# Attention in units of two batches by 64 tokens: one score tile, one value tile, two TensorE tasks per unit

## The chip, the cores and the metric

The kernel runs on one core of one Trainium2 chip. The metric is the time of one execution on the device in microseconds. Everything is float32 on the outside; the big matrix products are split into a high and a low part and run as three products each.

## The reference

The program is a linear-attention layer followed by a two-layer network. The attention keeps a state of 48 by 48 for each batch and head and walks over 768 tokens:

```
for t in range(S):                                  # B, H, S, D = 4, 8, 768, 48
    cur = einsum('bhd,bhe->bhde', u * kt, vt)
    y[:, :, t] = einsum('bhd,bhde->bhe', rt, state + cur)
    state = wt[..., None] * state + einsum('bhd,bhe->bhde', kt, vt)
x = y.transpose(0, 2, 1, 3).reshape(B * S, H * D)   # 3072 x 384
h = x @ w_in                                        # 384 x 2048
g = where(h > 0, h, exp(min(h, 0)) - 1)
out = g @ w_out                                     # 2048 x 384
```

## The kernel before, in words

The tokens are cut into six chunks of 128 (`NC = 6`). A unit is one chunk of one batch, so there are 24 units, four to a chunk. The network (called MLP below) runs once per chunk, over the 512 columns that the four units make, in 16 steps `f` of 128 hidden rows. A step is a block `g1` (9 matmuls of 128x512 into the tile `ph`, L238), two ScalarE passes and a VectorE pass for the nonlinearity (`r1`, `r2` L243 and L246, `stt` L249), the split into high and low (`gh` L253, `gl` L257), and a block `g2` (9 matmuls into three accumulators `acc`, L268). In the chunks 0 and 1 the first six steps run in two halves of 256 columns (`FH`), so that the network can begin when two units are done.

A unit of attention has these steps. VectorE makes the products of the decays from both ends of the segment by two scans (`e_scan` L377, `g_scan` L387) and multiplies them into r and k (`r_hat` L392, `k_hat` L396). The diagonal term u·r·k comes from TensorE in the units 0 to 7 (`diag_pe` L421) and from GpSimd in the others (L404, L407, then `diag` L411); it is spread to a diagonal matrix `am`, by eight ScalarE instructions in the units 0 to 7 (`spread_act` L432) and by GpSimd afterwards (`spread` L442). TensorE makes the scores (`score` L456, tile `pa_s`), VectorE copies the part above the diagonal into `am` (`mask` L460). TensorE transposes k (`trans` L465), ScalarE copies that out (L469). The values (`value`, L493 to L506) are the sum of the old state times r (`state_part`) and of v times `am`; ScalarE and VectorE take them out as the high and low part of x (`x_high` L513, `x_low` L519). The new state is k times v (`outer` L532), added to the decayed state (`scale_state` L472, `update` L540, for chunk 0 a copy, L542).

A unit comes in two forms. In the chunks 0, 1 and 5 the segment is 128 tokens long: scores of 128x128, the state part with contraction over 112 rows, then the product of k and v. In the chunks 2, 3 and 4 (`HALVES`) the unit is done in two segments of 64 tokens, one after the other: the scores are 64x64 in four corners of the array, and the state is updated twice, so that the order is `trans` and `score`, then `outer` and the state part of the first segment, then (after `update` and `scale_state`) the state part of the second segment and the masked values of both. In PSUM three banks (`SLOTS["pa"] = 3`) serve all of this: scores take two, a transpose one, values one or two. The state is stored as 96 columns per pair of heads (`st`, L326), of which each half of the rows uses 48 and the others stay zero, so that both heads of a pair are contracted at once over 112 rows.

The order of the work is written by a planner in the kernel (`Plan.order`, L94). It knows each task's engine, an estimated duration (`COST`), what it waits for, the buffers it takes, and due times derived from `BEGINS` (the start of each chunk's network). It simulates the engines, and the order it finds is issued as it stands: every engine then works its list in that order, and an instruction whose input is late holds up everything behind it on the same engine. Loads and stores stand in one list on SP. A guard (`guard` L579: a small matmul, two VectorE instructions) checks that the scans kept in range; a slow path behind a branch (`general`) runs if not.

The weights are converted at the start: 16 steps, each with one VectorE pass `conv_and` L563, two shifts L567 and L571, the low part L577, and two ScalarE passes L559 and L574.

Of the kernel before, what the change touches and what calls it, by code (L numbers as in the profile page):

```python
# [19 lines left out]
P = 128  # L20
C = 128
# [7 lines left out]
HC = C // 2  # L29
CWS = 2 * NP * (HC + 1)  # L30
W1, K1, R1 = CWS + 1, NP * C, NP * C
WKR = dict(w=(0, W1), k=(W1, W1 + K1), r=(W1 + K1, W1 + K1 + R1))
NU = NC * B
FH = (6, 6)
# [19 lines left out]
COST = dict(es=1.5, gs=1.4, pc=0.2, pd=0.6, md=0.22, spa=2.4, rh=0.62, kh=0.62, rk=0.48, rku=0.48, prk=1.1, prku=1.1, dg=0.5, mk=0.7, up=0.7, sc=0.5, xl=0.48,  # L54
            cand=0.5, cv=0.9, wl=0.9, stt=0.6, gl=0.64, fl=1.4, kt=0.5, xh=0.46, a=0.87, wh=0.8, r1=0.58, r2=0.6, gh=0.6,
            sp=1.7, s=1.15, t=0.5, v=1.75, v0=1.1, u=0.5, g=2.06, out=0.6, sh=0.6, ya=0.4, vh=1.0)
LAT = 0.06
DMA_FIRST, DMA_ISSUE, DMA_LAT, DMA_RATE = 1.0, 0.45, 1.9, 215.0
BEGINS = (20.9, 120.4, 207.5, 284.8, 361.5, 453.5, 461.1)
SOON = 0.0  # L60
HALF = 0.0
STAY = 0.0
SWITCH = 0.0
MODES = dict(s=1, v=2, u=3, pd=4)
STAG = 10.9
STAG_C = 0.0
HALVES = (2, 3, 4)
FIRST = "DVE"
FILL = {}
COLS = 128  # L70
PAD = 96
# [3 lines left out]
SLOTS = dict(w=2, k=3, r=3, rk=2, v=4, eg=2, md=2, am=2, kt=1, pa=3, wg=2, ph=2, m=2, gh=2, gl=2, x=2, acc=1, raw0=1, x0=1, x1=1, x1a=1, x1b=1)  # L75


class Plan:
# [15 lines left out]
    def order(self):  # L94
# [29 lines left out]
        server, mode = DMA_FIRST, None  # L124
# [5 lines left out]
        while len(order) < len(ts):  # L130
            moved = False
            for e in ready:
# [3 lines left out]
                for k in ready[e]:  # L136
# [6 lines left out]
                    u = (t["late"] + (STAY if e == "PE" and (k[0] in MODES) != (mode in MODES) else 0.0), rank[k])  # L143
# [22 lines left out]
                end = now + t["dur"] * (2.0 if e == "PE" and now < HALF else 1.0)  # L166
                if e == "PE":
                    end += SWITCH * (MODES.get(mode, 0) != MODES.get(k[0], 0))
                    mode = k[0]
# [46 lines left out]
ROUNDS = value_rounds()  # L216


def mlp(nc, w_h, w_l, ps_acc, ps_h, ml, gp, po, dst, last=False):
# [9 lines left out]
    def g1(s, x, fill=()):  # L229
# [3 lines left out]
        for m in fill:  # L233
            nc.tensor.matmul(ph[:, 0:P], m, m, start=True, stop=True)
# [57 lines left out]
def rwkv_elu_kernel(ctx, tc, wkr, rk, vp, u, uz, gkrw, gv, gu, w_in, w_out, out):  # L292
# [16 lines left out]
    ps_a = pool("ps_a", 3, space=PS)  # L309
# [10 lines left out]
    upper = kp.tile([P, C], F32, name="upper")  # L320
    upper_h = kp.tile([P, HC], F32, name="upper_h")
    upper_h4 = upper_h.bitcast(U32).unsqueeze(1).broadcast_to([P, 4, HC])
    upper4 = upper.bitcast(U32).unsqueeze(1).broadcast_to([P, 4, C])
# [4 lines left out]
    for u_ in units:  # L328
        u_["L"] = HC if u_["half"] else C
        u_["S"] = NP * C // u_["L"]  # L330
    spans = lambda x, u_: x.rearrange("d (s t) -> d s t", s=u_["S"])
    scan = lambda x, u_, z: spans(x[:, z, 0:u_["S"] * (u_["L"] + 1)], u_)
    raws, xts = {}, {}

    def set_reset(eng, u_):
        eng.memset(reset, 2.0 ** -62)
        eng.memset(scan(reset, u_, 0)[:, :, u_["L"]:u_["L"] + 1], 1.0)

    def constants():
        nc.scalar.preload_act_table_set("natural_log_exp_and_others")  # L340
        set_reset(nc.vector, units[0])
        nc.vector.memset(lim, -(2.0 ** 60))
        make_identity(nc, ident)
        nc.vector.memset(upper, 1.0)
        nc.gpsimd.affine_select(out=upper, in_=upper, pattern=[[1, C]], compare_op=ALU.is_gt,
                                fill=0.0, base=0, channel_multiplier=-1)
        nc.vector.memset(upper_h, 1.0)
        for z in range(2):
            nc.gpsimd.affine_select(out=upper_h[HC * z:HC * z + HC], in_=upper_h[HC * z:HC * z + HC], pattern=[[1, HC]], compare_op=ALU.is_gt,
                                    fill=0.0, base=0, channel_multiplier=-1)  # L350
        nc.gpsimd.memset(st, 0.0)
        nc.vector.memset(ones_c, 1.0)

    def warm():
        pw = ps_a.tile([P, P], F32, tag="pa", name="pw")
        for _ in range(WARM):
            nc.tensor.matmul(pw, ident, ident, start=True, stop=True)
# [4 lines left out]
    def load(u_, n):  # L362
        c, b = u_["c"], u_["b"]
        if n in WKR:
            lo, hi = WKR[n]
            t, src = ld.tile([R2, hi - lo], F32, tag=n, name=n, bufs=SLOTS[n]), wkr[c, b, :, lo:hi]
        elif n == "rk":
            t, src = ld.tile([P, 2, DM], F32, tag=n, name=n, bufs=SLOTS[n]), rk[c, b]
        else:
            t, src = ld.tile([P, 4 * P], F32, tag=n, name=n, bufs=SLOTS[n]), vp[c, b]  # L370
# [3 lines left out]
    def e_scan(u_):  # L374
        u_["eg"] = eg = at.tile([R2, 2, CWS], F32, tag="eg", name="eg", bufs=SLOTS["eg"])
        n = u_["S"] * (u_["L"] + 1)
        nc.vector.tensor_tensor_scan(out=eg[:, 0, 0:n][:, ::-1], data0=u_["w"][:, 1:n + 1][:, ::-1], data1=reset[:, 0, 0:n][:, ::-1],  # L377
                                     initial=0.0, op0=ALU.mult, op1=ALU.max)

    def decay(u_):  # L380
        u_["pc"] = at.tile([R2, 2 * NP, 1], F32, tag="pc", name="pc", bufs=6)[:, 0:u_["S"]]
        nc.scalar.copy(u_["pc"], scan(u_["eg"], u_, 0)[:, :, 0:1])

    def g_scan(u_):
        n = u_["S"] * (u_["L"] + 1)
        nc.vector.reciprocal(scan(reset, u_, 1)[:, :, 0:1], scan(u_["eg"], u_, 0)[:, :, 0:1])
        nc.vector.tensor_tensor_scan(out=u_["eg"][:, 1, 0:n], data0=u_["w"][:, 0:n], data1=reset[:, 1, 0:n],  # L387
                                     initial=0.0, op0=ALU.mult, op1=ALU.max)

    def r_hat(u_):  # L390
        r = spans(u_["r"].rearrange("d p t -> d (p t)"), u_)
# [464 lines left out]
```

## Time and profile before

| what | value |
|---|---|
| median of three runs | 541.48 us (539.18 to 541.5) |
| span of the profiled execution | 540.9 us |
| TensorE matmul busy | 515.5 us (95%) |
| VectorE busy | 371.1 us (69%) |
| ScalarE busy | 285.8 us (53%) |
| GpSimd busy | 74.7 us (14%) |
| matmuls of the network, L238 and L268, of the chain that ended last | 34% and 33% |

The page of the profile cuts the span in 40 slices and gives each engine's busy share in tenths. A timeline row gives start, duration, engine, line, operation and shape (contraction rows times output rows, then operand), and how many instructions of one kind it joins. A matmul's duration in a row includes the way through the array, so consecutive rows overlap; what an instruction occupies is the distance from its start to the start of the next row. A float32 matmul shows as two records, a transpose and the network's matmuls as one. The chain of waits follows the work that ended last back in time.

### The profile page before, as it was taken

How to read it: one execution, taken by the hardware profiler on the slowest of the kernel's cores; microseconds unless marked ns; L12 is line 12 of the kernel's file. 1: busy time of each engine (PE TensorE's matmuls, PEld its weight loads, DVE VectorE, ACT ScalarE, POOL GpSimd, SP SyncE). 2: the span in 40 equal slices, each digit the busy share in tenths (PEclk: the TensorE clock that was granted, in tenths of full speed). 3: DMA queues.
4: the chain of work that ended last, by engine and by line, in shares of the span. 5: the costliest groups of instructions: out<-in, count | busy, mean ns of one | idle time of the engine just before them, and what ended most of it. 6: DMA issues, size and time to landing. Idle time of an engine off the chain costs nothing.

```text
span 540.9 us, 12202 instructions
## 1 busy us (share of the span) xinstructions
PE 515.5 (95%) x5121; PEld 427.7 (79%) x5121; DVE 371.1 (69%) x614; ACT 285.8 (53%) x570; POOL 74.7 (14%) x102
## 2 busy tenths in 40 slices
PE   6876999989999999999999999999999999999994
PEld 5666998878999777787777788777788887888883
DVE  5899899988778875469964478964436995333331
ACT  3768588675855453455453365543355543454441
POOL 2000000000243120028120035120031400000000
PEclk9977899979999999999999999999999999999998
DMA  8954754021562200094310083100084110010001
GB/s 243 287 176 141 226 175 164 19 56 35 175 178 76 65 2 2 2 263 133 85 33 2 3 241 103 35 2 3 1 254 124 48 35 2 0 60 0 1 0 63
DMA packets 26749, 47.54 MB, mean 88 GB/s; under 512 B 2753, under 2 KB 9281, under 8 KB 26689
## 3 DMA queue, kind: packets, MB, share of 16 engines
q1 hardware_dynamic: 26544, 46.58, 28.7%
q8 instruction: 42, 0.69, 0.5%
q14 instruction: 19, 0.15, 0.1%
q10 hardware_dynamic: 144, 0.13, 0.1%
HBM read 41.98 MB, written 4.72 MB: 86 GB/s over the span
## 4 chain that ended last, share of the span: by engine, by line
PE 80%; DVE 9%; DMA 6%; ACT 2%; issue 1%; SPq 0%; DVEq 0%; ACTq 0%
PE ph L238 34%; PE acc L268 33%; PE pa_s L456 3%; PE pa_y L501 3%; DMA v<-in_vp_dram 3%; PE pa_u L506 2%; PE pa_u L493 2%; PE pa_u L532 1%; DMA wrawx<-in_w_out_dram 1%; DMA rk<-in_rk_dram 1%; PE pa_t L465 1%; DVE eg L387 1%; DVE gl L257 1%; DMA k<-in_wkr_dram 1%; DVE r L392 1%
## 5 line engine op out<-in xcount | busy, mean ns | idle before, releaser
L243 ACT ACTIVATE m<-ph 128x512 f32<-128x512 f32 (+1 forms) x108 | 59.2, 549 | 132.8 <-PE ph L238 131.5
L249 DVE SCALAR_TENSOR_TENSOR m<-m,ph 128x512 f32<-128x512 f32 (+1 forms) x108 | 67.4, 624 | 84.7 <-ACT m L246 84.2
L238 PE MATMUL ph<-xh,w_h 128*128 128x512 f32 (+1 forms) x324 | 123.2, 380 | 2.0 <-ACT w_h L574 1.6
L238 PE MATMUL ph<-xh,w_l 128*128 128x512 f32 (+1 forms) x324 | 120.7, 372 | 3.7 <-DVE w_l L577 3.7
L268 PE MATMUL acc<-gh,w_h 128*128 128x512 f32 (+1 forms) x325 | 123.6, 380 | 0.0
L268 PE MATMUL acc<-gl,w_h 128*128 128x512 f32 (+1 forms) x325 | 120.2, 370 | 0.1
L238 PE MATMUL ph<-xl,w_h 128*128 128x512 f32 (+1 forms) x324 | 120.1, 371 | 0.0
L268 PE MATMUL acc<-gh,w_l 128*128 128x512 f32 (+1 forms) x325 | 119.9, 369 | 0.0
L257 DVE TENSOR_TENSOR gl<-m,gh 128x512 fp32r<-128x512 f32 (+1 forms) x108 | 73.2, 681 | 36.4 <-ACT gh L253 35.9
L253 ACT CAST gh<-m 128x512 fp32r<-128x512 f32 (+1 forms) x108 | 61.5, 571 | 55.9 <-DVE m L249 33.2
L238 PEld LDWEIGHTS ph<-xh,w_l 128*128 128x128 f32 x324 | 62.3, 192 | 15.0 <-DVE w_l L577 4.6
L238 PEld LDWEIGHTS ph<-xh,w_h 128*128 128x128 f32 x324 | 62.2, 192 | 14.3 <-ACT w_h L574 2.4
L268 PEld LDWEIGHTS acc<-gh,w_h 128*128 128x128 f32 x325 | 62.4, 192 | 12.8 <-issue 1.0
L268 PEld LDWEIGHTS acc<-gh,w_l 128*128 128x128 f32 x325 | 62.4, 192 | 10.2
L268 PEld LDWEIGHTS acc<-gl,w_h 128*128 128x128 f32 x325 | 62.5, 192 | 9.7 <-DVE gl L257 0.5
L238 PEld LDWEIGHTS ph<-xl,w_h 128*128 128x128 f32 x324 | 62.5, 193 | 9.4
L246 ACT ACTIVATE m<-m 128x512 f32<-128x512 f32 (+1 forms) x108 | 63.3, 586 | 2.9
L442 POOL TENSOR_SCALAR_AFFINE_SELECT am<-md 64x256 f32<-64x256 f32 (+1 forms) x56 | 30.5, 548 | 96.9 <-PE pa_u L493 61.9
L404 POOL TENSOR_TENSOR rk<-rk 128x384 f32<-128x384 f32 x16 | 19.1, 1192 | 134.1 <-DMA rk<-in_rk_dram 132.2
L377 DVE TENSOR_TENSOR_SCAN eg<-w,reset 112x516 f32<-112x516 f32 (+1 forms) x24 | 31.0, 1292 | 2.6 <-DMA w<-in_wkr_dram 2.6
L456 PE MATMUL pa_s<-r,k 48*64 48x64 f32 (+1 forms) x576 | 27.3, 262 | 5.5 <-ACT md L425 2.2
L401 ACT ACTIVATE junk<-eg,lim 112x1032 bf16<-112x1032 f32 (+1 forms) x24 | 27.7, 1153 | 8.2 <-DVE eg L387 8.2
(72 smaller groups left out, 513.4 us busy)
## 6 DMA issues: line engine op xcount, KB each, us to landing
v<-in_vp_dram SPq DMA_DIRECT2D x24, 256.0 KB, 6.5
rk<-in_rk_dram SPq DMA_DIRECT2D x16, 384.0 KB, 4.1
w<-in_wkr_dram SPq DMA_DIRECT2D x24, 227.9 KB, 3.9
k<-in_wkr_dram SPq DMA_DIRECT2D x24, 224.0 KB, 4.9
r<-in_wkr_dram SPq DMA_DIRECT2D x24, 224.0 KB, 5.3
out_dram<-o SPq DMA_DIRECT2D x17, 256.0 KB, 2.5
wrawx<-in_w_in_dram SPq DMA_DIRECT2D x10, 384.0 KB, 3.5
wrawx<-in_w_out_dram SPq DMA_DIRECT2D x10, 384.0 KB, 4.1
```

The lines of the kernel that those rows point to most:

```text
L238: nc.tensor.matmul(ph[z:z + COLS], w[:, f, 0, k, z:z + COLS], x_[:, k, :], start=(k == n == 0), stop=(k == NK - 1 and n == 2))
L243: act(s["m"], s["ph"], AF.Relu, scale=-1.0)
L246: act(s["m"], s["m"], AF.Exp, scale=-1.0)
L249: stt_(s["m"], s["m"], -1.0, s["ph"], ALU.add, ALU.max)
L253: nc.scalar.copy(s["gh"], s["m"])
L257: nc.vector.tensor_tensor(s["gl"], s["m"], s["gh"].bitcast(F32), ALU.subtract)
L268: nc.tensor.matmul(a_[z:z + COLS], w[:, f, 1, m, z:z + COLS], g[:, s_], start=(f == n == 0 and lo == 0), stop=(f == NF - 1 and q == parts ...
L377: nc.vector.tensor_tensor_scan(out=eg[:, 0, 0:n][:, ::-1], data0=u_["w"][:, 1:n + 1][:, ::-1], data1=reset[:, 0, 0:n][:, ::-1], initial=0. ...
L401: act(junk[:, :, 0:n], u_["eg"][:, :, 0:n], AF.Relu, bias=lim, accum_out=flags[:, u_["i"]:u_["i"] + 1])
L404: eng.tensor_tensor(u_["rk"][:, 0], u_["rk"][:, 0], u_["rk"][:, 1], ALU.mult)
L442: nc.gpsimd.affine_select(out=am[rs, :, 0:L], in_=u_["md"][rs, q::2].unsqueeze(2).broadcast_to([L, NP, L]), pattern=[[0, NP], [1, L]], com ...
L456: nc.tensor.matmul(pa[q][ts, p, 0:L], u_["k"][rs, p, ts], u_["r"][rs, p, ts], start=True, stop=True)
```

## The change

Every unit is now a pair of batches times 64 tokens. There are 12 steps in time of two units each, still 24 units, and four units still make one chunk of 512 columns. The two segments of a unit belong to two batches, so they do not depend on each other; the dependence runs from unit i to unit i+2, also within a chunk. The units 0 and 1 have no old state (`first`), the units 22 and 23 make no new one (`last`).

- One TensorE task `s` makes the transposes of k and the scores; one task `v` makes the state part, the masked values and the product of k and v. Before there were three or four tasks: `t`, `s`, `v`, `u`, and `ya` in the halved form.
- PSUM: a tile of two banks, one buffer (`pair`, tag `pa`), holds the scores, and then the values and the state product together; another tile of one bank, one buffer (`single`, tag `pb`), holds the transposes, the diagonal term, and the guard's sum. The task `s` takes both, `v` takes `pa` again after the mask, and holds it until `x_high`, `x_low` and `update` are done.
- The state is 80 columns wide (`st`), with 48 in use at the same place for both heads of a pair. The state part is contracted over the 48 rows of one head, 32 output rows at a time: 32 matmuls in place of 24, in two passes with a TensorE `drain` between them, since the second pass adds to the same PSUM places from the other half of the array's rows.
- One `mask`, one `x_high`, one `x_low`, one `scale_state` and one `update` instruction per unit, each over both segments. `update` of the units 0 and 1 is a copy on ScalarE. The spread on ScalarE writes 64 columns instead of 128 per instruction; GpSimd spreads with two instructions instead of four.
- The constants for both segment lengths, and the reset of them by GpSimd when the length changes, are gone. Costs, due times (`BEGINS`, a spacing `STAG` of 17 instead of 10.9) and the guard's due time are new; the guard's old due time lay behind those of the whole last chunk.
- The host lays the inputs out per unit; sizes of loads are the same.

```diff
-    st = cst.tile([R2, B, NP, 2 * D], F32, name="st")
-    units = [dict(c=i // B, b=i % B, i=i, half=i // B in HALVES) for i in range(NU)]
+    st = cst.tile([R2, B, NP, 80], F32, name="st")
+    sv = st[:, :, :, 16:16 + D]
+    units = [dict(c=i // B, b=(2 * (i % STEP), 2 * (i % STEP) + 1), i=i, first=i < STEP, last=i >= NU - STEP) for i in range(NU)]
...
+    def pair():
+        return ps_a.tile([P, 2, 512], F32, tag="pa", name="pa", bufs=1)
+
+    def single():
+        return ps_a.tile([P, 512], F32, tag="pb", name="pb", bufs=1)
...
     def score(u_):
-        u_["pa"] = pa = [ps_a.tile([P, NP, C], F32, tag="pa", name="pa_s") for q in range(2)]
...
+        if not u_["last"]:
+            u_["pt"] = pt = single()[:, 0:NP * R2].rearrange("t (p d) -> t p d", p=NP)
+            for p in range(NP):
+                nc.tensor.transpose(pt[:, p], u_["k"][:, p, :], ident[0:R2, 0:R2])
+        u_["pa"] = pa = pair()[:, :, 0:NP * L].rearrange("t q (p s) -> t q p s", p=NP)
...
+    def mask(u_):
+        nc.vector.copy_predicated(u_["am"], upper4, u_["pa"])
...
+    def scale_state(u_):
+        b = slice(u_["b"][0], u_["b"][0] + 2)
+        tt(sv[:, b], sv[:, b], u_["pc"].rearrange("d (p h) o -> d h p o", h=2).broadcast_to([R2, 2, NP, D]), ALU.mult)
+
+    def value(u_):
+        v, am, rp = u_["v"], u_["am"], u_["r"]
+        both = pair()
+        u_["pu"] = pu = both[0:R2, :, 0:NP * D].rearrange("d h (p e) -> d h p e", p=NP)
+        u_["py"] = py = both[:, :, NP * D:NP * D + NK * L].rearrange("d h (k t) -> d h k t", k=NK)
...
+        def state_part(swap):
+            for n in range(2 * NP):
+                for h in range(2):
+                    p, x = HEADS[h ^ swap][n]
+                    rs, e = slice(64 * (x // 2), 64 * (x // 2) + D), (16, 48, 0, 32)[x]
+                    mm(h, p, x, st[rs, u_["b"][h], p, e:e + 32], rp[rs, p, L * h:L * h + L])
+
+        if not u_["first"]:
+            state_part(1)
+            nc.tensor.drain()
+            state_part(0)
+        for p, x in ROUNDS:
+            for h in range(2):
+                rs = slice(L * h, L * h + L)
+                mm(h, p, x, v[rs, P * p + 32 * x:P * p + 32 * x + 32], am[rs, x // 2, p], stop=u_["last"] and (p, x) in ENDS)
+        if u_["last"]:
+            return
         for p in range(NP):
...
             for h in range(2):
+                rs = slice(L * h, L * h + L)
+                for z in range(2):
+                    m = 64 - 16 * z
+                    nc.tensor.matmul(pu[64 * z:64 * z + m, h, p], u_["kt"][rs, p, 64 * z:64 * z + m], v[rs, P * p + 80 * z:P * p + 80 * z + D],
+                                     start=False, stop=(p == NP - 1))
...
-        hold("pa", ("s", i), [("mk", i, 0), ("mk", i, 1)], 2, fifo=False)
...
+        hold("pa", ("s", i), [("mk", i)], fifo=False)
+        hold("pb", ("s", i), [("kt", i)], fifo=False)
+        hold("kt", ("s", i), [("v", i)])
+        hold("pa", ("v", i), [("xh", i), ("xl", i), ("up", i)], fifo=False)
...
-    add(("guard",), "PE", 0.3, guard, [("fl", i) for i in range(NU)], due=BEGINS[-2] + 15)
+    add(("guard",), "PE", 0.3, guard, [("fl", i) for i in range(NU)], due=BEGINS[-2] + 10.0)
```

More of the change, by code (lines that the diff above doesn't have):

```diff
@@ L33 @@
 NU = NC * B
+STEP = B // 2
 FH = (6, 6)
@@ L165, in order @@
                         users.setdefault(x, []).append(h)
[L166 to L169, printed above, removed]
+                end = now + t["dur"]
                 busy[e] = end
@@ L216 @@
 ROUNDS = value_rounds()
+ENDS = {(3 * p + (0, 1, 1, 2)[x]) % 4: (p, x) for p, x in ROUNDS}.values()
+HEADS = [[(p, 2 * z + x) for x in range(2) for p in range(NP)] for z in range(2)]
 def mlp(nc, w_h, w_l, ps_acc, ps_h, ml, gp, po, dst, last=False):
@@ L535, in update @@
-    def update(u_, h=0):
-        for z in range(2):
-            rs = slice(64 * z, 64 * z + D)
-            sv = st[rs, u_["b"], :, D * z:D * z + D]
-            if u_["c"] > 0:
-                tt(sv, sv, u_["pu"][h][rs], ALU.add)
-            else:
-                (nc.scalar.copy if FIRST == "ACT" else nc.vector.tensor_copy)(sv, u_["pu"][h][rs])
+        xh, xl = (columns(u_, t) for t in xts[u_["c"]])
+        tt(xl, u_["py"], xh.bitcast(F32), ALU.subtract)
+    def update(u_):
+        b = slice(u_["b"][0], u_["b"][0] + 2)
+        if not u_["first"]:
+            tt(sv[:, b], sv[:, b], u_["pu"], ALU.add)
+        else:
+            (nc.scalar.copy if FIRST == "ACT" else nc.vector.tensor_copy)(sv[:, b], u_["pu"])
@@ L629, in rwkv_elu_kernel @@
             add(("sp", i), "POOL", K["sp"], lambda u_=u_: spread(u_), [("md", i)], lock=True)
-        add(("s", i), "PE", K["sh" if u_["half"] else "s"], lambda u_=u_: score(u_), [("rh", i), ("kh", i), ("sp", i)])
-        for q in range(2):
-            add(("mk", i, q), "DVE", K["mk"] * (0.55 if u_["half"] else 1.0), lambda u_=u_, q=q: mask(u_, q), [("s", i), ("sp", i)])
-        if c < NC - 1:
-            add(("t", i), "PE", K["t"], lambda u_=u_: trans(u_), [("kh", i), ("const",)])
-            add(("kt", i), "ACT", K["kt"], lambda u_=u_: trans_out(u_), [("t", i)])
@@ L636, in rwkv_elu_kernel @@
-        after = [("mk", i, 0), ("mk", i, 1), ("ld_v", i)]
-        if c > 0:
-            before = ("up2" if c - 1 in HALVES else "up", i - B)
-            add(("sc", i), "DVE", K["sc"], lambda u_=u_: scale_state(u_), [("pc", i), before], lock=True)
+        add(("s", i), "PE", K["s"], lambda u_=u_: score(u_), [("rh", i), ("kh", i), ("sp", i), ("const",)])
+        add(("mk", i), "DVE", K["mk"], lambda u_=u_: mask(u_), [("s", i), ("sp", i)])
+        if not u_["last"]:
+            add(("kt", i), "ACT", K["kt"], lambda u_=u_: trans_out(u_), [("s", i)])
@@ L653, in rwkv_elu_kernel @@
-        add(("xh", i), "ACT", K["xh"] + more, lambda u_=u_: x_high(u_), [("v", i)])
-        add(("xl", i), "DVE", K["xl"] + more, lambda u_=u_: x_low(u_), [("xh", i)])
-        if c < NC - 1 and not u_["half"]:
-            add(("u", i), "PE", K["u"], lambda u_=u_: outer(u_), [("kt", i), ("v", i)])
-            add(("up", i), "DVE" if c else FIRST, K["up"], lambda u_=u_: update(u_), [("u", i)])
+        add(("v", i), "PE", K["v0" if u_["first"] else "v"], lambda u_=u_: value(u_), after,
+            due=BEGINS[c] - (B - 1 - i % B) * STAG - 2.0 if c > 1 else None)
@@ L658, in rwkv_elu_kernel @@
+        add(("xh", i), "ACT", K["xh"], lambda u_=u_: x_high(u_), [("v", i)])
+        add(("xl", i), "DVE", K["xl"], lambda u_=u_: x_low(u_), [("xh", i)])
+        if not u_["last"]:
+            add(("up", i), FIRST if u_["first"] else "DVE", K["up"], lambda u_=u_: update(u_), [("xl" if u_["first"] else "xh", i)])
     for f in range(NF):
```

295 lines of the change are left out of this document (102 added, 193 removed).

## The prediction

> **What bounds the kernel now.** I read the page first, then the busy time by windows, then TensorE's timeline in one unit of each form, the groups of VectorE by shape, and the chain of waits where TensorE is not full.
>
> ```profile
> span 540.9 us, 12202 instructions
> PE 515.5 (95%) x5121; PEld 427.7 (79%) x5121; DVE 371.1 (69%) x614; ACT 285.8 (53%) x570; POOL 74.7 (14%) x102
> ...
> DVE  5899899988778875469964478964436995333331
> ...
> PEclk9977899979999999999999999999999999999998
> ```
>
> TensorE is busy 95% of the span, so after the start every microsecond of matmul time that goes is a microsecond of the end. The first four slices (13.5 us each) are different: VectorE stands at 8 and 9 tenths and the clock is not full. The windows say how full VectorE is there, and what is lost around 110 us:
>
> ```profile
> 23.00:53.00 30.00, 21.68 (x174) 18.76 (x170) 29.51 (x46) 22.68 (x51) 0.00 (x0) 0.81 0.51 161
> ...
> 110.14:122.54 12.40, 10.22 (x68) 8.64 (x67) 10.58 (x17) 8.86 (x26) 0.00 (x0) 0.72 0.23 60
> ```
>
> Columns after the length are busy PE, PEld, DVE, ACT, POOL, then the granted clock. From 23 to 53 us VectorE works 29.51 of 30.00 us: it sets the pace, and TensorE waits for converted weights. From 110 to 122 us TensorE has a hole and then a clock of 0.72.
>
> So there are three places to cost: TensorE's work per unit, VectorE's work per unit up to 53 us, and the hole.
>
> **TensorE, one unit.** A halved unit before (chunk 2), from its transposes to the next unit's:
>
> ```profile
> 177.39 0.55 PE L465 MATMUL pa_t<-ident,k 112*128 112x112 f32 x4
> 177.87 0.69 PE L456 MATMUL pa_s<-r,k 48*64 48x64 f32 x32
> 178.50 0.50 PE L268 MATMUL acc<-gh,w_h 128*128 128x512 f32 x1
> ...
> 180.79 0.57 PE L532 MATMUL pa_u<-v,kt 64*48 64x48 f32 x32
> 181.30 0.54 PE L506 MATMUL pa_u<-r,st 112*32 112x64 f32 x24
> 181.77 0.50 PE L238 MATMUL ph<-xh,w_h 128*128 128x512 f32 x1
> ...
> 184.05 0.54 PE L506 MATMUL pa_u<-r,st 112*32 112x64 f32 x24
> 184.53 0.86 PE L493 MATMUL pa_u<-am,v 64*32 64x64 f32 x64
> 185.31 0.50 PE L268 MATMUL acc<-gh,w_h 128*128 128x512 f32 x1
> ...
> 189.55 0.55 PE L465 MATMUL pa_t<-ident,k 112*128 112x112 f32 x4
> ```
>
> The network's undisturbed pace, and the hole, stand in the chain of waits:
>
> ```profile
> 87.85 4.08 PE ph L238 x18
> ...
> 111.31 2.44 ACT am L432 x8
> ...
> 114.65 2.08 PE pa_s L456 x16
> 116.73 3.88 PE ph L238 x9
> ```
>
> A block of nine is 4.08/2 = 2.04 us. Between 177.39 and 189.55, 12.16 us, lie four blocks, so the unit costs 12.16 - 8.16 = 4.00 us. By distances of starts its pieces are: transposes 0.48, scores 0.63, state product 0.51, state part 0.47 twice, masked values 0.78; together 3.34. The other 0.66 is three visits at 0.22 each: the first network matmul after a visit takes longer, and there is a gap before the next visit.
>
> A unit after has the same transposes and scores, 1.11. For `v` I need the pace inside a piece and its end. A record's own duration is the second number:
>
> ```profile
> L506 PE MATMUL pa_u<-r,st 112*32 112x64 f32 x576 | 13.0, 223 | 0.2 <-DVE st L472 0.2
> L493 PE MATMUL pa_u<-am,v 64*32 64x64 f32 x768 | 10.3, 223 | 0.0
> ```
>
> The last of the 64 masked records starts at 184.53 + 0.86 - 0.22 = 185.17, so 63 steps take 0.64, 10 ns each, and the change of array mode before the next row takes 0.14. The 24 state records step in 0.32, 14 ns each, with 0.16 at the end. After, the masked values are the same 64 records, 0.64. The state part becomes 32 matmuls of 48 rows by 32 outputs, 64 records over two row halves and four column groups as in the masked values: 0.64 by that row. The state product keeps its 32 records, 0.51 with its end. With one mode change, 0.64 + 0.64 + 0.14 + 0.51 = 1.93, plus the drain. Two visits at 0.22 add 0.44. So a unit costs 1.11 + 1.93 + 0.44 = 3.48 us plus the drain.
>
> The drain between the passes has no row. Below, it could cost nothing more than an ordinary record. The nearest row is the change of array mode, 0.14 at an end of a piece. Starting again behind an emptied array costs at most about half of a visit's 0.22, so one emptying and one restart are 0.25, and I take that; the upper end is twice as much, 0.5. A unit is then 3.73.
>
> The Trainium skill says (TensorEngine Tiling (Array Packing), Key Properties) that a change of tiling mode drains TensorE; by that alone the drain would cost the 0.14 of a mode change, and the 22 units with a drain would gain 2.4 us more than I sum below.
>
> Chunks 2 to 4: 12 units x (4.00 - 3.73) = 3.2 us saved. A unit of the full form, in chunk 1:
>
> ```profile
> 143.74 0.55 PE L465 MATMUL pa_t<-ident,k 112*128 112x112 f32 x4
> 144.22 1.16 PE L456 MATMUL pa_s<-r,k 48*128 48x128 f32 x16
> 145.31 0.38 PE L268 MATMUL acc<-gh,w_h 128*128 128x256 f32 x1
> ...
> 146.58 0.86 PE L501 MATMUL pa_y<-r,st 112*32 112x128 f32 x24
> ...
> 148.25 0.39 PE L268 MATMUL acc<-gh,w_h 128*128 128x256 f32 x1
> ...
> 153.51 0.56 PE L532 MATMUL pa_u<-v,kt 128*48 128x48 f32 x16
> 154.01 0.60 PE L465 MATMUL pa_t<-ident,k 112*128 112x112 f32 x4
> ```
>
> Transposes 0.48, scores 1.09, values 1.67, state product 0.50: 3.74, and two visits, since the product rides with the next transposes: 4.2. Chunk 1 saves 4 x (4.2 - 3.73) = 1.9. Chunk 5 had no transposes and no state product, 1.09 + 1.67 + 0.44 = 3.20 for each of four units, 12.8; now its first two units must make a state for the last two: 2 x 3.73 + 2 x (0.63 + 0.64 + 0.64 + 0.14 + 0.25 + 0.44 = 2.74) = 12.9. It loses 0.1. In chunk 0 the units 2 and 3 gain a state part (0.64 + 0.25) and lose about as much in scores (0.46) and one visit: even.
>
> **VectorE at the start.** The groups by shape (mean ns is the last number before the bar's right side):
>
> ```profile
> L540 DVE TENSOR_TENSOR st<-st,pa_u 48x192 f32<-48x192 f32 x56 | 19.5, 348 | 6.1 <-PE pa_u L506 5.7
> L472 DVE TENSOR_TENSOR st<-st,pc 112x384 f32<-112x384 f32 x32 | 18.8, 592 | 0.5
> ...
> L460 DVE COPY_PREDICATED am<-upper,pa_s 128x512 f32<-128x512 uint32 x24 | 16.1, 725 | 3.5 <-PE pa_s L456 3.5
> ...
> L460 DVE COPY_PREDICATED am<-upper_h,pa_s 128x256 f32<-128x256 uint32 x24 | 9.3, 439 | 14.3 <-PE pa_s L456 14.2
> ...
> L519 DVE TENSOR_TENSOR xl<-pa_y,xh 128x384 fp32r<-128x384 f32 x12 | 6.6, 550 | 3.1 <-ACT xh L513 3.1
> ...
> L542 DVE COPY st<-pa_u 48x192 f32<-48x192 f32 x8 | 2.8, 353 | 0.8 <-PE pa_u L532 0.7
> ```
>
> A full unit had two masks of 725 ns; it has one. The copies of the state (2 x 353 ns in each of units 0 and 1) go to ScalarE, which is busy 22.68 of those 30 us and can hide two of about 0.55 (the `xl` shape); if it can't, they return, 1 us. The units 2 and 3 gain a `scale_state`, 0.59 each. Up to 53 us, with three masks on the way: 3 x 0.73 + 4 x 0.35 - 2 x 0.59 = 2.4 us less on the engine that sets the pace. I take 2.1. Later VectorE saves too (a halved unit had two masks of 439, two scalings and four updates, now one mask, one scaling and one update of about 0.57), but there it is not the bound.
>
> **The hole at 110 us.** TensorE waits for ScalarE's spread (2.44), then runs the scores at half clock (2.08 against 1.09) and the next block in 3.88 against 2.04: 2.4 + 1.0 + 1.8 = 5.2 us lost. The spread gets shorter (half the columns) and VectorE, which feeds the weights of the last steps, arrives earlier. Whether TensorE then has a block to run is the planner's choice. Bounds: nothing, and all 5.2; I take 2.
>
> **The end.** The guard is last on TensorE and VectorE, ahead of the copies of the last output:
>
> ```profile
> 533.36 0.15 PE pf L581 x2
> ...
> 533.53 0.18 DVE tot L583
> ...
> 533.84 1.02 DVE o L280 x2
> ```
>
> Its due time now lies inside the last chunk; 533.84 - 533.36 = 0.5 us go.
>
> **Sum**, against the profiled span: 540.9 - 3.2 - 1.9 + 0.1 - 2.1 - 2.0 - 0.5 = 531.3. The median of the runs is 0.6 above that span, so I predict 532. GpSimd's spread, the loads and SP's list keep their sizes; GpSimd at 14% and the DMAs have room.
>
> **Rivals.**
>
> *The single tiles serialize (slower).* PSUM had three slots; now the scores of unit i+1 wait until mask i, or `x_high`, `x_low` and `update` of unit i, are done, and the transposes wait for the one-bank tile. A TensorE that waits holds every network block behind it. Per unit the exposed chain is the mask 0.73, then `x_high` about 0.5, `x_low` 0.55 and `update` 0.57, with hand-overs some 2.7 us. With due times 17 us apart and blocks of 2.04 to fill, it is hidden in chunks 2 to 5. In units 0 to 5 the network lacks weights and VectorE's list is full: six units exposed are 16.2 us against the 9.6 saved: 548. It decides from 1.6 us of exposed waiting per unit on. For it: VectorE's 29.51 of 30.00. Against: until 53 us TensorE waits anyway.
>
> *The drain or the new 48x32 form is dearer.* With 0.5 for the drain, 22 units lose 5.5 of the gain: 537. If the state part runs at the pace of the 112-row one, 14 ns a record, it costs 0.25 more in each: 537 as well; both together, 543. From 0.69 for the drain on nothing is left.
>
> *The early gains don't come.* VectorE's time is taken by something else and the hole stays: 532 + 4.1 = 536.
>
> *Small matmuls have a floor.* If each of the 64 state records took 25 ns where the masked values take 10, the part would cost 1.6 in place of 0.64, and 22 units would add 21 us: 553. The Trainium skill (TensorE: Matmul & The Clock Gate, the section on 56 against 53.3 ns) states such a floor of about 25 ns from start to start; the 64 records in 0.78 us above contradict it for tiles that share the array, so it gets 1 in 50.
>
> **How the numbers follow.** Forecast 0.57; single tiles 0.16; drain or form 0.12; no early gain 0.13; floor 0.02. The range: below, all of the hole (3.2 more), a drain at 0.1 (3.3 more) and 0.5 for the rest give 525; above, 544 takes in the dear drain and half of the single tiles' case. About 0.5%, 2.7 us, is what a measurement here can tell, so faster means under 538.8. From forecast 0.56, from no early gain 0.12, from the drain 0.06: faster 0.74. Same: 0.04 from the drain, 0.03 from single tiles, 0.03 from the others: 0.10. Slower 0.16.
>
> **What would show it.** In the changed profile: a steady unit (its two visits, from one `s` to the next less the blocks of 2.04 between) at 3.6 to 3.9; the gap between the two passes of the state part near 0.25; the state part's records some 10 ns apart; TensorE's busy time about 8 us shorter; VectorE still full to some 50 us with the first scores of units 2 and 3 about 2 us earlier; no row of the guard behind the last block. Wrong would be: TensorE waiting for `x_low`, `update` or a mask in chunks 2 to 5, more idle time on TensorE than the 25.4 us (540.9 - 515.5) of before, or a gap at the drain over 0.5.

## The result, and the profile after

The changed kernel takes 557.11 us (median of 6, 554.04 to 557.83), the kernel before beside it 541.49: a ratio of 1.0269, 95% interval 1.0227 to 1.0312. It is slower by 15.6 us; 532 was forecast. The profiled execution of the changed kernel is the fastest of its six (554.04, span 552.3), so its trace shows 11.4 us of the loss. First the head of its page:

```profile
span 552.3 us, 14893 instructions
...
PE 512.0 (93%) x6537; PEld 426.8 (77%) x6537; DVE 348.8 (63%) x524; ACT 283.0 (51%) x564; POOL 74.0 (13%) x75
...
DVE  5889589998659873358953368872368863323331
```

TensorE's busy time fell by 3.5 us (515.5 to 512.0), not by 8. Its idle time rose from 25.4 to 40.3 (552.3 - 512.0). So the loss is waiting. To see where, both executions are cut where the same share of the network is done (36, 288, 576 and 1152 of 1728 full-width matmuls). Columns: length, busy PE, PEld, DVE, ACT, POOL, granted clock, DMA share, GB/s. Before:

```profile
0.00:48.20 48.20, 35.17 (x259) 31.18 (x260) 40.06 (x64) 29.56 (x69) 2.79 (x10) 0.90 0.73 215
48.20:131.50 83.30, 78.99 (x634) 68.80 (x634) 76.18 (x120) 56.88 (x113) 0.00 (x0) 0.92 0.39 123
131.50:225.80 94.30, 94.30 (x1346) 79.91 (x1344) 68.52 (x132) 51.27 (x120) 20.10 (x28) 1.00 0.24 72
225.80:390.00 164.20, 163.57 (x2018) 130.05 (x2017) 112.77 (x192) 78.68 (x150) 37.00 (x48) 1.00 0.26 75
390.00:540.90 150.90, 143.49 (x871) 117.74 (x869) 73.63 (x108) 69.43 (x120) 14.84 (x16) 0.99 0.17 53
```

After:

```profile
0.00:51.30 51.30, 35.22 (x424) 32.19 (x424) 41.05 (x63) 31.65 (x78) 2.72 (x11) 0.93 0.67 202
51.30:133.70 82.40, 75.91 (x938) 65.81 (x937) 72.52 (x113) 55.55 (x120) 0.00 (x0) 0.94 0.40 124
133.70:234.50 100.80, 95.33 (x1742) 81.56 (x1740) 62.16 (x100) 46.75 (x104) 21.43 (x18) 0.98 0.25 74
234.50:397.20 162.70, 160.41 (x2145) 130.09 (x2144) 100.27 (x144) 78.59 (x142) 31.88 (x30) 1.00 0.25 71
397.20:552.30 155.10, 145.13 (x1295) 117.18 (x1293) 72.83 (x106) 70.42 (x122) 17.98 (x16) 0.99 0.18 52
```

Length less busy PE is TensorE's idle time: 13.0, 4.3, 0.0, 0.6, 7.4 before; 16.1, 6.5, 5.5, 2.3, 10.0 after. The worst is the third stretch, chunk 1, where before had no idle time at all. The second and the fourth (chunks 2 and 3) got shorter, by 0.9 and 1.5 us; but in the second, after has done one unit's values less, which it does in the third.

Who TensorE waited for, after (total us, times, longest):

```profile
PE pa L489 <- issue: 5.3, 3, 2.5
PE pb L411 <- ACT md L415: 4.6, 1, 4.6
PE pa L464 <- issue: 4.2, 22, 0.2
PE pa L464 <- ACT st L511: 3.1, 1, 3.1
PE pb L436 <- issue: 2.7, 1, 2.7
PE acc L260 <- DVE gl L249: 2.6, 5, 0.9
...
PE ph L230 <- DVE m L241: 1.4, 3, 0.8
PE pa L464 <- DVE am L445: 1.4, 1, 1.4
PE acc L260 <- ACT gh L245: 1.0, 2, 0.7
```

In the same view of before, the longest row is for converted weights, and no row is for `gl`, `gh` or `m`:

```profile
PE ph L238 <- DVE w_l L577: 3.7, 3, 1.9
```

The third row of after is the drain, 22 times. The first is new: three stops in the middle of the state product (L489); "issue" means that the view shows nothing that TensorE waited for. This is the longest of the three:

```profile
56.24 0.66 PE L489 MATMUL pa<-v,kt 64*64 64x48 f32 x12
59.38 0.88 PE L489 MATMUL pa<-v,kt 64*64 64x48 f32 x20 [2.48 <-issue]
```

The second and fourth rows are single tiles in units 0 and 1.

A steady unit and the next, timeline of TensorE:

```profile
251.05 0.55 PE L436 MATMUL pb<-ident,k 112*128 112x112 f32 x4
251.53 0.69 PE L442 MATMUL pa<-r,k 48*64 48x64 f32 x32
...
254.42 0.45 PE L464 MATMUL pa<-r,st 48*32 48x64 f32 x32
255.06 0.46 PE L464 MATMUL pa<-r,st 48*32 48x64 f32 x32 [0.19 <-issue]
255.46 0.85 PE L464 MATMUL pa<-am,v 64*32 64x64 f32 x64
256.24 0.68 PE L489 MATMUL pa<-v,kt 64*64 64x48 f32 x32
...
267.18 0.55 PE L436 MATMUL pb<-ident,k 112*128 112x112 f32 x4
```

From 251.05 to 267.18 are 16.13 us with 54 network matmuls, six blocks of 2.04: the unit costs 3.89. State part and masked values take 256.24 - 254.42 = 1.82. With 0.22 as one record's own duration, the last record of the first pass starts at 254.42 + 0.45 - 0.22 = 254.65 and the next pass at 255.06: 0.41 at the drain, of which 0.19 shows as idle. Each pass of 32 records takes about 0.24, under 8 ns a record. Ahead of the masked values is another gap of 0.16, and they take 0.78 with the change of array mode behind them.

### The profile page after: what moved, and what is told of

Same layout as the page of the kernel before. It is cut to its first block, busy times and chain, and to the rows that moved or that the text cites. A ratio compares the mean times of both kernels' runs of the same rounds, so it can differ in the third digit from the quotient of the medians.

```text
span 552.3 us, 14893 instructions
## 1 busy us (share of the span) xinstructions
PE 512.0 (93%) x6537; PEld 426.8 (77%) x6537; DVE 348.8 (63%) x524; ACT 283.0 (51%) x564; POOL 74.0 (13%) x75
## 4 chain that ended last, share of the span: by engine, by line
PE 77%; DVE 9%; issue 4%; ACT 4%; DMA 3%; SPq 1%; ACTq 0%; DVEq 0%
PE acc L260 32%; PE ph L230 31%; PE pa L464 7%; PE pa L489 3%; PE pa L442 2%; DMA w<-in_wkr_dram 1%; DVE gl L249 1%; PE pb L436 1%; DVE m L241 1%; DMA r<-in_wkr_dram 1%; ACT am L421 1%; PE pb L411 1%; DVE eg L378 1%; DVE wg L540 1%; DVE wg L536 1%
## 5 line engine op out<-in xcount | busy, mean ns | idle before, releaser
L230 PEld LDWEIGHTS ph<-xh,w_h 128*128 128x128 f32 x324 | 63.4, 196 | 13.2 <-DVE m L241 2.0
L230 PEld LDWEIGHTS ph<-xh,w_l 128*128 128x128 f32 x324 | 63.5, 196 | 10.8 <-DVE w_l L546 0.8
L427 POOL TENSOR_SCALAR_AFFINE_SELECT am<-md 64x512 f32<-64x512 f32 x32 | 31.1, 972 | 74.3 <-DVE reset L377 43.4
L369 DVE TENSOR_TENSOR_SCAN eg<-w,reset 112x520 f32<-112x520 f32 x24 | 30.5, 1270 | 6.0 <-DMA w<-in_wkr_dram 6.0
L391 ACT ACTIVATE junk<-eg,lim 112x1040 bf16<-112x1040 f32 x24 | 27.8, 1158 | 8.9 <-DVE eg L378 8.9
L378 DVE TENSOR_TENSOR_SCAN eg<-w,reset 112x520 f32<-112x520 f32 x24 | 31.6, 1319 | 0.8
```

The lines of the kernel that those rows point to most:

```text
L230: nc.tensor.matmul(ph[z:z + COLS], w[:, f, 0, k, z:z + COLS], x_[:, k, :], start=(k == n == 0), stop=(k == NK - 1 and n == 2))
L369: nc.vector.tensor_tensor_scan(out=eg[:, 0][:, ::-1], data0=u_["w"][:, 1:CWS + 1][:, ::-1], data1=reset[:, 0][:, ::-1], initial=0.0, op0=A ...
L378: nc.vector.tensor_tensor_scan(out=u_["eg"][:, 1], data0=u_["w"][:, 0:CWS], data1=reset[:, 1], initial=0.0, op0=ALU.mult, op1=ALU.max)
L391: act(junk, u_["eg"], AF.Relu, bias=lim, accum_out=flags[:, u_["i"]:u_["i"] + 1])
L427: nc.gpsimd.affine_select(out=am[rs].rearrange("t q p s -> t (q p) s"), in_=u_["md"][rs].rearrange("t q p -> t (q p)").unsqueeze(2).broadc ...
```

## The experiments

All start from the changed kernel unless they say otherwise; each time is a median of at least four runs, each ratio is to the kernel before, with its interval.

**A second drain.** In each unit with a state part:

```
             state_part(0)
+            nc.tensor.drain()
```

> The changed kernel with a second drain on TensorE in each of the 22 units with a state part, between the two state passes and the masked values; nothing else is changed, not even the order of the work. Theory 'the drain is dear': the gap of 0.40 us at the drain in the trace after is the price of emptying and restarting TensorE, so each further drain costs the same, 22 x 0.40 = 8.8 us: about 566. Rival 'the gap belongs to the change of tiles, not to the drain': the second drain, with the same tile form on both sides, costs no more than 0.1 us in each unit, so the time is 557 to 559 and no second gap is seen.

Measured: 568.81, ratio 1.0479 [1.0449, 1.0510]. In its timeline the same piece reads:

```profile
235.93 0.45 PE L464 MATMUL pa<-r,st 48*32 48x64 f32 x32
236.57 0.46 PE L464 MATMUL pa<-r,st 48*32 48x64 f32 x32 [0.19 <-issue]
237.36 0.85 PE L464 MATMUL pa<-am,v 64*32 64x64 f32 x64 [0.33 <-issue]
238.14 0.68 PE L490 MATMUL pa<-v,kt 64*64 64x48 f32 x32
```

From its first record to the product are 2.21 us instead of 1.82: the second drain costs 0.39. That is 8.6 in 22 units, and the time rose by 11.7, so the drain is dear as the theory had it, and the rival falls; the other 3 us were not taken apart (the stops are of other lengths there). The Trainium skill (TensorEngine Tiling (Array Packing), Key Properties) says that a change of tiling mode drains TensorE; here such a change (from the masked values to the product) took 0.14 to 0.15, while the drain that the program orders took 0.39 to 0.41.

**The state part without a drain.**

```
-    st = cst.tile([R2, B, NP, 80], F32, name="st")
+    st = cst.tile([R2, B, NP, 2 * D], F32, name="st")
...
+            for n in range(NK * NP):
+                for h in range(2):
+                    k, j = divmod(n, 4)
+                    nc.tensor.matmul(py[32 * j:32 * j + 32, h, k], st[:, u_["b"][h], n // 3, 32 * (n % 3):32 * (n % 3) + 32],
+                                     rp[:, n // 3, L * h:L * h + L], start=(h, j) not in opened, stop=False)
```

> The changed kernel with the state kept as two diagonal blocks again (112 rows by 96 columns a pair of heads, the other columns zero), so that the state part is 24 matmuls of 112 rows instead of 32 of 48 rows, in one pass without a drain; the update becomes two operations of 48 rows, the scaling covers 96 columns. Same order of the work. Theory 'the drain is dear': a unit's state part goes from 64 records at 10 ns and a gap of 0.40, 1.04 us, to 48 records at 14 ns and a change of tiles of 0.14, 0.81 us: 22 x 0.23 = 5 us less, of which VectorE's 0.5 us a unit more may take 1 or 2 back in chunks 0 and 1: 552 to 554. Rival 'the cost per unit is not in the drain': no gain, 557 or above by VectorE's additional work.

Measured: 556.65, 1.0267 [1.0206, 1.0329]: no gain that can be told. The piece did get shorter, but TensorE's waits for VectorE grew:

```profile
255.14 0.93 PE L477 MATMUL pa<-r,st 112*32 112x64 f32 x48
256.00 0.86 PE L463 MATMUL pa<-am,v 64*32 64x64 f32 x64
256.79 0.68 PE L491 MATMUL pa<-v,kt 64*64 64x48 f32 x32
```

```profile
PE acc L260 <- DVE gl L249: 4.3, 5, 1.6
PE ph L230 <- DVE m L241: 4.0, 3, 1.6
```

256.79 - 255.14 = 1.65 instead of 1.82, 3.7 us in 22 units. But VectorE is 21.5 us busier (370.3), and TensorE's waits for `gl` and `m` rose from 4.0 to 8.3. All of these 8.3 us lie behind 51 us, so VectorE does matter in the later chunks.

**More tiles at the start.** Two forms. In the first, the plan's order is kept:

```
-        u_["pd"] = pd = single()[:, 0:NS]
+        u_["pd"] = pd = (ps_h.tile([P, N], F32, tag="ph", name="ph_d") if u_["first"] else single())[:, 0:NS]
...
-            (nc.scalar.copy if FIRST == "ACT" else nc.vector.tensor_copy)(sv[:, b], u_["pu"])
+            nc.vector.tensor_copy(sv[:, b], u_["pu"])
```

> The changed kernel with two edits for units 0 and 1: the diagonal term's matmuls write a tile of the network's pool, so that they no longer wait for the one-bank tile, and the copy of the state stands on VectorE instead of ScalarE, where it is queued behind eight operations of the spread. Theory 'the single tiles serialize the start': the first network block starts at about 27 us again instead of 31.5, and the time falls by 4 to 5 us: 552 to 553. Rival 'VectorE's weight conversions pace the start': the first block comes earlier, but the blocks after it wait for their weights, so less than 2 us is left at 110 us and the time is 555 to 557.

In the second, the plan knows of it: diagonal terms of units 0 and 1 and transposes of unit 1 in the accumulators' banks, `FIRST = "DVE"`, and the copy due behind `x_high`.

> The changed kernel with more tiles at the start alone: the diagonal terms of units 0 and 1 and the transposes of unit 1 write the banks of the first accumulators, which are not in use yet, and the copy of the state of units 0 and 1 stands on VectorE and is due as soon as x_high is done. Theory 'the single tiles serialize the start': the first network block starts at 27 to 28 us instead of 31.5, and 3 to 5 us of that are left at 110 us; in sum 552 to 554. Rival 'the weights pace the start': the first block is early, but the ninth half block is no earlier than before the edit, and the time is 556 to 558.

Measured: 557.45, 1.0279 [1.0236, 1.0322], and 552.67, 1.0184 [1.0147, 1.0221]. In the first form the first network block came even later (32.54 instead of 31.49). The second gained 4.4 in the median, but not by its theory: its first network block came at 31.10, 36 matmuls' worth of network was done at 52.8 instead of 51.3, and 252 at 118.9 instead of 118.2. The freed TensorE waits elsewhere, and VectorE waits more in 8 to 54 us:

```profile
DVE rkc L406 <- DMA r<-in_wkr_dram: 4.3, 2, 2.6
DVE xl L504 <- ACT xh L500: 3.7, 2, 1.9
```

In the changed kernel these rows are 1.6 and 1.8. The span of the profiled execution is 0.8 shorter (551.5), and what it gained it gained in chunks 3 and 4, whose order the new plan changed too. Single tiles at the start are therefore not shown to be a cause, and where the rest of the 4.4 us comes from stays open.

**Where TensorE's instructions stand.** 128 drains ahead of TensorE's first matmul, then 18 in the 4.65 us in which it waits for the tile of unit 1:

```
+        for _ in range(128):
+            nc.tensor.drain()
         pw = single()[:, 0:P]
```

> The changed kernel with 128 drains on TensorE ahead of its first matmul, where it has nothing to do; they move every later instruction by half a block of 16 KB of TensorE's instruction queue. Theory 'TensorE runs out of instructions': the stalls of 2.5, 1.1 and 1.8 us inside the value matmuls at 57, 136 and 160 us go with the blocks of the instruction queue, so they vanish there or come up elsewhere; if all vanish the time falls by up to 5 us to 552, if as many come up elsewhere it stays. Rival 'they wait for data': the same three stalls stand at the same matmuls, and the time is 557.

> The changed kernel with 18 drains on TensorE ahead of the diagonal term of unit 1, in the 4.65 us in which TensorE waits there anyway. In the kernels so far every stall inside the value matmuls began at the TensorE instruction whose number is 193 or 194 over a multiple of 256, and only visits of v (320 instructions) that hold two such borders, at offsets up to 54 and 256 more, stalled. Moved by 18, the visits of units 5 and 7 that stalled at 136 and 160 us hold one border or two of which the first lies in the first 6 instructions, unit 2 (57 us) the same, and the unit at 309 us holds its second border in its last instruction. Theory 'instruction blocks': the three stalls, 5.3 us in the trace after, vanish but for less than 1 us, and the time falls by 4 to 5 us to 552 to 553. Rival 'it is data, or chance': the three stalls stay, 556 to 558.

Measured: 560.79, 1.0361 [1.0299, 1.0423], and 562.52, 1.0392 [1.0333, 1.0451]. The 128 drains take 8.5 us, 66 ns each, of which 1.7 are left at the first network block. For these runs I counted TensorE's instructions in the trace, weight loads and matmuls included, up to each stop:

| kernel | stops in small matmuls: instruction number (us idle) |
|---|---|
| changed | 1218 (2.48), 3009 (1.08), 4033 (1.76) |
| 128 in front | 1730 (0.94), 5826 (1.64), 6337 (1.63) |
| 18 in front | 1218 (4.02), 3009 (0.93), 4033 (1.91), 8386 (1.32) |

Two more stops over 0.5 us stood in the network's matmuls, at 4802 (1.35) with 128 in front and at 7873 (0.74) with 18. Every number is 193 or 194 over a multiple of 256 (call such a place a border), and each time a packet of 16 KB on the queue of TensorE's instructions began at most 1.8 us before the stop, or within it. The changed kernel has 53 such packets for 13,168 instructions: about one for each 256.

The traces of all 18 kernels of this document say more. Count the packets: the k-th belongs to the border at 256 k + 193. At none of their 872 borders did TensorE go on earlier than 1.23 us after the end of that border's packet, and each of the 56 stops over 0.4 us that stand at borders ended 1.23 to 1.68 us after it (the one at 59.38: the packet ended at 58.01). From the start of a packet to its border were never less than 2.2 us, and no packet started more than 297 instructions ahead of it. So a stop is a late packet: TensorE used up the instructions that it had before the next ones were there. What makes one packet start later than another is open.

With 128 in front, the three old stops are gone (0.40 is left at 4033), and 360 matmuls' worth of network was done 4.5 us earlier than in the changed kernel (163.6 instead of 168.1) although the start was later: the stops are on the path. Three others came up in small matmuls. The shift by 18 moved other matmuls under the same numbers, and they stopped at the same numbers: my rule for a safe place (a border in the first 6 instructions of a visit of `v` does no harm) was wrong, the mechanism held.

**The product as a task of its own.**

```
+        if not u_["last"]:
+            add(("u", i), "PE", 0.6, lambda u_=u_: product(u_), [("v", i)], due=plan.tasks[("v", i)]["due"] and plan.tasks[("v", i)]["due"] + 2.0)
```

> The changed kernel with one part undone: the state product is a TensorE task of its own again, behind v, so that the plan can put network blocks between the two, which it does in 11 of the 22 units (those of units 2, 6 and 8 among the first ones, while units 3, 4, 5 and 7 stay in one piece); x_high comes after it. Theory 'instruction blocks in long visits': where a network block stands between, no stall is seen; the 57 us stall (2.5 to 4.9 us so far) goes, and a stall is left only in visits that are still whole. Against it stand 11 visits more at 0.22, 2.4 us. In sum 1 to 3 us less: 554 to 556. Rival 'the stall of the product waits for data (kt, v)': it still stands ahead of the product wherever it stood, and the time is 558 or above.

Measured: 555.93, 1.0290 [1.0228, 1.0352], within the interval of the changed kernel. The telling row is at 60 us, where the plan put network between values and product:

```profile
57.47 0.28 PE L230 MATMUL ph<-xh,w_l 128*128 128x256 f32 x1
59.94 0.39 PE L230 MATMUL ph<-xh,w_h 128*128 128x256 f32 x1 [2.19 <-issue]
```

It is number 1218 again, and now a matmul of the network, on the tiles that the three before it had just used. So the stop follows the instruction's number and not the data: the rival falls. That a block of network prevents it was wrong as well; the twelve half-width matmuls that stood ahead of the stop, 1.4 us, were not enough.

**The order at the end.**

```
-BEGINS = (20.9, 120.0, 206.0, 285.0, 364.0, 443.0, 509.0)
+BEGINS = (20.9, 120.0, 206.0, 285.0, 364.0, 443.0, 450.6)
```

> The changed kernel with the due times of the last chunk as close as they were in the kernel before (0.475 us apart instead of 4.125), so that the last three second halves of the network follow the last first half. Theory 'the order at the end costs': the waits of TensorE for the last gh and gl (0.9 us) and for the g2 holes in the last 70 us go: 1 to 2 us less, 555 to 556. Rival 'the end is hidden or noise': no change, 557.

Measured: 556.83, 1.0256 [1.0212, 1.0299]: no difference that can be told. From 1440 matmuls' worth of network to the last it took 65.5 us instead of 67.0, as expected; but in the profiled execution a new stop of 1.5 at 474 us (number 12482, again 194 over) stood ahead of that stretch.

**The hole of before alone**, `SPREAD = ["ACT"] * 4 + ["POOL"] * 20` in the kernel before.

> The kernel before, with the spread of units 4 to 7 on GpSimd instead of ScalarE. It bounds what the hole at 110 us (TensorE waits 2.44 for ScalarE's spread, then runs at the clock 0.72) is worth by itself, which the change was forecast to win: if the hole is the spread's, 2 to 5 us less than the kernel before, 537 to 540; if only the order or the late weights make it, no change, 541 to 543.

Measured: 542.05, 1.0008 [0.9982, 1.0034]. The hole stayed (2.79 us idle ahead of the scores at 114): it is not the spread's.

**The spread off GpSimd.**

```
-SPREAD = ["ACT"] * 8 + ["POOL"] * 16
+SPREAD = ["ACT"] * 24
```

> The changed kernel with the spread of the diagonal term on ScalarE in every unit, where units 8 to 23 had it on GpSimd. In the trace after, VectorE's k_hat takes 1.51 and 1.13 us beside a spread on GpSimd instead of 0.68, and TensorE then waits for gl (0.77 us at 332, 0.91 at 414; 2.6 us over the run, nothing before). Theory 'GpSimd slows VectorE and the network's gl comes late': those waits fall below 1 us in sum, and the time by 1.5 to 2.5 us, 554.5 to 555.5. Rival 'the multiplications on GpSimd do the same, or ScalarE's gh is late instead, behind eight operations of the spread': no less than 1 us is gained, 556 to 559.

Measured: 550.6, 1.0149 [1.0116, 1.0183], the best of all here, and more than expected. What suggested it is this stretch of the changed kernel, VectorE and then GpSimd:

```profile
329.46 0.68 DVE L383 TENSOR_TENSOR r<-r,eg 112x512 f32<-112x512 f32 x1
330.07 1.51 DVE L387 TENSOR_TENSOR k<-k,eg 112x512 f32<-112x512 f32 x1
331.50 1.00 DVE L453 TENSOR_TENSOR st<-st,pc 112x384 f32<-112x384 f32 x1
332.43 0.68 DVE L249 TENSOR_TENSOR gl<-m,gh 128x512 fp32r<-128x512 f32 x1
```

```profile
329.87 1.16 POOL L394 TENSOR_TENSOR rk<-rk 128x384 f32<-128x384 f32 x1 [3.08 <-DMA rk<-in_rk_dram]
330.98 2.64 POOL L427 TENSOR_SCALAR_AFFINE_SELECT am<-md 64x512 f32<-64x512 f32 x2
```

`k_hat`, 0.69 in the median, takes 1.51 beside GpSimd, and `gl` behind it comes late. With the spread on ScalarE the waits for `gl` fell from 2.6 to 0.5, those for `gh` and `m` from 2.4 to 1.5:

```profile
PE acc L260 <- DVE gl L249: 0.5, 2, 0.3
```

But the plan's order changed as well, and `k_hat` stayed at 874 ns in the mean (907 in the changed kernel): its long ones now stand beside the multiplications that GpSimd kept:

```profile
139.36 1.50 DVE L387 TENSOR_TENSOR k<-k,eg 112x512 f32<-112x512 f32 x1
```

```profile
140.39 1.34 POOL L397 TENSOR_TENSOR rk<-rk,ub 128x384 f32<-128x384 f32 x1
```

In these two kernels and in the one before, no `r_hat` or `k_hat` without GpSimd beside it took more than 0.69, and all longer ones had it beside them. The kernel before had such long ones too: its 48 `r_hat` and `k_hat` took 37.7 us together, against 40.4 in the changed kernel and 39.7 here. So GpSimd does hold them up, but their length alone does not explain the gain. The next run changes GpSimd's operations alone: the spread is again on GpSimd, in four operations of 64x256 as in the halved units of before, with engines and order untouched.

```
+            for q in range(2):
+                nc.gpsimd.affine_select(out=am[rs, q], in_=u_["md"][rs, q].unsqueeze(2).broadcast_to([L, NP, L]),
```

> The changed kernel with GpSimd's spread in four operations of 64 x 256 elements a unit, as before the change, instead of two of 64 x 512; engines, plan and order are the changed kernel's. Theory 'long operations of GpSimd hold VectorE up, and the network's gl comes late': VectorE's k_hat falls from 907 ns in the mean towards the 741 of before, TensorE's waits for gl fall from 2.6 us, and the time falls by 1 to 3 us: 554 to 556. Rival 'the run with the spread on ScalarE gained by its other order of the work': k_hat, the waits and the time stay as they are, 556 to 558.

Measured: 554.78, 1.0233 [1.0210, 1.0257].

```profile
L387 DVE TENSOR_TENSOR k<-k,eg 112x512 f32<-112x512 f32 x24 | 19.7, 821 | 0.0
```

```profile
PE ph L230 <- DVE m L241: 2.4, 3, 1.2
...
PE acc L260 <- DVE gl L249: 1.1, 3, 0.5
```

`k_hat` is halfway back (907 to 821, with 741 before), the waits for `gl` fell from 2.6 to 1.1, the time is 2.3 less, as the theory said; but the waits for `m` rose from 1.4 to 2.4, and the intervals overlap, so the 2.3 are not clear of noise. The lock that one engine takes is in the Trainium skill (SBUF — State Buffer, SBUF: two separate sides: VectorE and GpSimd share a pair of ports, and who has it keeps it for the whole instruction); the 1.51 beside 0.69 agrees. How much of the 6.5 us that the spread on ScalarE gained is this, and how much the order, stays open.

**Combinations.** Start and end; start and product; start and spread on ScalarE; these two and the state part without a drain; spread on ScalarE and 26 drains in the wait of unit 1.

> The start with more tiles (552.7 by itself) together with the close due times at the end, whose last 67 us were 1.5 us shorter by themselves. If both are real and add up: 551 (550 to 552). If the order at the end is only moved about: 552 to 554. In this plan the guard stands ahead of the last block's last matmuls.

> The start with more tiles together with the state product as a task of its own. If the start (4.4 us less by itself) and the stalls in long visits are two separate losses: the sum of both, 549 to 551. If the plan with three tasks brings its own waits, 553 or above.

> The start with more tiles (4.4 us less by itself) and the spread on ScalarE in every unit (6.5 us less by itself), together. If the waits of the first units and the late gl are two separate losses, both are saved: 546 (545 to 548). If either gain only came from another order of the work and not from the waits named, they don't add up: 549 to 552.

> The two edits of the run beside it, and the state part in one pass of 112 rows without a drain (its costs in the plan adapted). In the first trial of that state part its values and state part together came to 1.65 us a unit instead of 1.82, but VectorE's additional work made gl late. Theory 'the drain's price is real and its removal was hidden by the late gl': with the spread off GpSimd 22 x 0.17 = 3.7 us come through: 542 to 544. Rival 'VectorE's 1 us more a unit in chunks 0 and 1 sets the pace again': no gain over the run beside it, 546 to 549.

> The spread on ScalarE (550.6) with 26 drains in the wait ahead of the diagonal term of unit 1. By the numbers of TensorE's instructions the three visits that stalled (5.7 us in that trace) then hold one border of 256 each, at 255, 236 and 254 of their 320 instructions, and the unit at about 309 us holds two. Theory 'a stall needs two borders in one visit': at 57, 134 and 159 us nothing is left but one stall of 1.3 us later: 546 to 548. If what counts is the number of small instructions since the last border, with the scores in front of v counting too, the stalls shrink to about 1 us each: 548 to 550. Rival 'chance': 550 to 553.

Measured: 553.0 [1.0120, 1.0249], 554.12 [1.0162, 1.0277], 553.67 [1.0170, 1.0274], 552.61 [1.0131, 1.0239], 555.99 [1.0222, 1.0275]. No two gains add up, and none comes near the kernel before. The last one tells most: at 1218, 3009 and 4033 it stops again (2.82, 1.22, 2.17), now in the masked values, with one border in the visit; two more of over 1.5 came later, at 7873 in the network and at 8385. So two borders in one visit are not needed. The fourth again gains nothing that can be told from the missing drain.

## Why the prediction was wrong, step by step

- *The unit.* 3.89 us, where 3.73 was forecast and 3.6 to 3.9 allowed. The drain is 0.41 (taken 0.25, bounds 0 to 0.5), the product 0.60 (0.51). Twelve units then save 12 x (4.00 - 3.89) = 1.3 and not 3.2, chunk 1 saves 4 x (4.2 - 3.89) = 1.2 and not 1.9. The mechanism was right, the size of the drain was off. That the rest of the state part came out as forecast, 0.64, is luck: its records ran under 8 ns apart and not 10, but the sum had left out the gap of 0.16 ahead of the masked values.
- *The pace of a piece, taken from shorter visits.* This is the step that failed first. Each piece of `v` was costed from visits of before with at most 88 matmul records. The new `v` has 160, with their weight loads 320 instructions in 2.4 us, and three visits stopped for 5.3 us, all before 162 us, for packets of instructions that came late; with 128 instructions in front these stops went and others came. No trace of before has a stop over 0.4 us at a border, and the prediction had no term and no rival for it: it put the stops at nothing.
- *"Later VectorE saves too (...), but there it is not the bound."* The second step that failed. TensorE waited 5.0 us for `gl`, `m` and `gh`, all of it past 51 us, where the same view of before has no row for such data. VectorE's average of 63% hides that a chain of `r_hat`, `k_hat` and the scaling can stand ahead of `gl` on its list, as at 329 us.
- *VectorE at the start.* Its work from 8 to 54 us fell from 42.62 to 40.57, 2.05 where 2.1 was forecast. But its idle time grew by the same 2.05: it now waits for `x_high` (1.8), a load (1.6) and `m` (1.3). Nothing was left.
- *The hole at 110 us* is gone, as hoped: TensorE is busy 24.2 of the 25 us from 110 to 135, at the full clock (22.8 at 0.86 before). The stop at 57 us and the later start had already cost more.
- *The end.* The guard is off it, but the last `g2` waits for `gh` (0.69 at 542): about even at best.
- *The rivals.* Single tiles: their waits are there, 4.6 and 3.1 us in units 0 and 1, and the time came out on their side; but taking them away gave nothing at the start, and in chunks 2 to 5 no wait for `x_low`, `update` or a mask is seen, as forecast. The dear drain was part of it. The early gain at the start did not come, as that rival had it, but the hole went. The floor of 25 ns is not there.

TensorE's 14.9 us more of idle time: 5.3 stops, 4.2 drains (22 x 0.19), 3.1 in the first 51 us; the remaining 2.3 are the waits for the network's data less those of before that went (the hole among them). Against this stand 3.5 us less work. The stops and the drain's price are shown by experiments, though no run took the stops away without bringing others; the late `gl` is shown in part; that the first 51 us belong to VectorE's list is read from the traces and not isolated. Of the 4.2 us between the 11.4 of the traces and the 15.6 of the medians, 3.1 are the scatter between executions (554.04 and the median 557.11), and the stop at 57 us alone was 2.48 to 4.87 in the runs that kept the order there; the rest lies outside the spans.

## What to carry to other kernels

Cost a merged visit of many small matmuls by its instructions, not only by its pace: 256 of them in 2 us were at times more than TensorE's instruction queue delivered here, where a packet of 256 needed at least 2.2 us from its start to its first use. An engine that is 63% busy can still be late at one place: look at what stands ahead of the operation that the bottleneck waits for. And work saved on a full engine is a gain only if its next operation is ready, so trace what it will wait for instead.

## What the runs showed of the hardware

- Behind dense small matmuls TensorE stopped at instructions numbered 193 or 194 over a multiple of 256, for 0.4 to 4.9 us, whether product, values or network stood there, and went on 1.23 to 1.68 us after the end of a 16 KB packet of its instruction queue. Not every dense visit stops: with the spread on ScalarE one with borders at its instructions 7 and 263 ran through in 2.45 us; the second border's packet had ended 1.82 us ahead of it.
- A drain within a unit's small matmuls cost 0.39 to 0.41 us, the change from 64x32 to 64x64 tiles 0.14 to 0.15; 128 drains in a row took 66 ns each.
- VectorE's multiplication of 112x512 elements took 0.68 to 1.51 us, the long ones beside GpSimd.
